# The first input tile of a fused SSM and SwiGLU kernel: one load of 128 rows, or two halves of 64 rows on two DMA queues

## The chip, the cores and the metric

The kernel adds a state space model (SSM) and a gated feed-forward block (SwiGLU) to its input. It runs on one core of a Trainium2 chip. The metric is device time in microseconds (us). "Before" had a median of 179.36 us in three runs (179.34 to 179.51).

The engines are named as in the profile. PE is TensorE (PEld its weight loads), DVE is VectorE, ACT is ScalarE, POOL is GpSimd, and SP is SyncE. A "q" after a name (SPq, ACTq, POOLq) is that engine's instruction queue, from which it also issues DMAs.

## The reference, cut to what matters

```python
def reference(A_x, ..., B_w_gate, B_w_up, B_w_down):
    xn = _layernorm(A_x, axis=-1)          # x is 2048 rows of 512, bf16
    return A_x + _A_ref(xn, ...) + _B_ref(xn, B_w_gate, B_w_up, B_w_down)

def _B_ref(x, w_gate, w_up, w_down):       # 512 -> 1376 -> 512
    return (silu(x @ w_gate) * (x @ w_up)) @ w_down
# _A_ref: a diagonal complex state space scan between two dense projections
```

## The kernel before

The rows are handled in 16 tiles of 128 rows, four to a chunk. Almost all of the time is dense matmul work. This is about the first 13 us, the head. There the first four tiles are loaded, normalised, transposed on TensorE and multiplied with the gate weights one tile ("quarter") at a time, so that TensorE can begin as soon as tile 0 is there.

```python
def x_load(a, **kw):                       # one tile: 128 rows of 1 KB
    return dma("ld_x%d" % a, x_sb[:, a:a + 1, :], x_v[:, a:a + 1, :], [("x", a)], TILEB, **kw)
def wg_load(nm, k0, k1, **kw):             # 128 rows of gate weights per k
    return dma("ld_wg" + nm, wg[:, k0:k1, 0:FG], wg_v[:, k0:k1, 0:FG], [("wg", nm)], ...)

g.add("pool", lambda e: e.memset(prow[:], 0.0), writes=[("prow0",)], name="prow0", est=100)
x_load(0)                                                            # SyncE's queue
x_load(1)
act_q = [dma("ld_touch", tch[0:16], wg_v[0:128:8, :, 0:2], [("tch",)], 16 * 16, eng="act")]
act_q.append(wg_load("a0", 0, 2, eng="act", order=(act_q[-1],)))     # ScalarE's queue
x_load(2)
act_q.append(wg_load("a1", 2, 3, eng="act", order=(act_q[-1],)))
wg_load("a2", 3, 4)
x_load(3)
# ... (parameters, the other weights, tiles 4 to 15)
# PE: 11 warm-up matmuls on constants, transposes of tile 0, 18 gate matmuls
#     of tile 0, transposes of tile 1, ... until 112 are done; then full width
```

The touch reads 256 bytes of the gate weights and nobody uses them. "a0" is the first part of the gate weights (448 KB); the first gate matmul waits for it as well as for tile 0.

## Time and profile before

| what | value | where it is read |
|---|---|---|
| PE busy | 98% of a span of 177.5 us | the page's busy table |
| x tile 0 (x0) complete | 3.10 us | issue at 0.79 plus 2.3 us to landing |
| gate part a0 complete | 5.03 us | issue at 1.23 plus 3.8 us to landing |
| first transposes of tile 0 | 5.00 us | the timeline |
| first gate matmul | 5.83 us | the timeline |
| first full-width gate matmul | 12.94 us | the timeline |

The page has these two lines, the busy time of the engines and the shares of the chain of waits that ended last:

```profile
PE 173.5 (98%) x935; PEld 83.7 (47%) x935; DVE 162.7 (92%) x284; ACT 88.0 (50%) x116; POOL 11.7 (7%) x22
...
PE 96%; DMA 1%; DVE 1%; ACT 1%; issue 0%
```

TensorE bounds the kernel, so only its late start can be shortened. The chain of waits in order of time (columns: start, duration, what) shows that start:

```profile
0.79 2.31 DMA x_sb<-in_A_x_dram
...
3.12 0.71 DVE st L530
...
4.92 0.61 ACT xn_sb L548
...
5.58 0.28 PE pb L582 x2
5.86 0.11 PE pb L477
5.97 1.02 PE pb L803 x18
```

The chain begins with x0's load, goes through the layer norm and then stays on PE. Line 582 is the transposes and line 803 the gate matmuls.

The view of one tile's instructions, narrowed to the first issue, gives the time an issue holds the queue (in ns: minimum, median, maximum) and the time from issue to landing. First x0, then a0:

```profile
L402 SPq DMA_DIRECT2D x_sb<-in_A_x_dram x1: 393/393/393, 0.8 to 0.8; - x1
DMA to landing us min/median/max: 2.3/2.3/2.3
...
L402 ACTq DMA_DIRECT2D wg<-in_B_w_gate_dram x1: 448/448/448, 1.2 to 1.2; - x1
DMA to landing us min/median/max: 3.8/3.8/3.8
```

Issuing x0 holds SyncE's queue for 0.393 us. Gate part a0 is issued at 1.23 us, right behind the touch, and is there 0.8 us before the first gate matmul.

### The profile page before, as it was taken

The numbers are of one execution on the slowest core, as the hardware profiler recorded it, in microseconds if no ns is written. First come the engines' busy times: TensorE is split into PE (matmuls) and PEld (weight loads), VectorE is DVE, ScalarE is ACT, GpSimd is POOL, SyncE is SP. The second block draws the span as 40 slices with busy tenths as digits, with TensorE's granted clock in tenths as the row PEclk, the third lists the DMA queues.
The fourth block names the chain that finished last, engine by engine and source line by source line (L and its number), as shares of the span: only waits on it lengthen the run. The fifth ranks groups of instructions, "written<-read, shape, count | busy, mean of one in ns | idle before, by whom it ended". The sixth has DMA issues, their size and how long they took to land.

```text
span 177.5 us, 2429 instructions
## 1 busy us (share of the span) xinstructions
PE 173.5 (98%) x935; PEld 83.7 (47%) x935; DVE 162.7 (92%) x284; ACT 88.0 (50%) x116; POOL 11.7 (7%) x22
## 2 busy tenths in 40 slices
PE   7899999999999999999999999999999999999994
PEld 3794444444444444444444444444444444444743
DVE  2966999699999999999999999999999999999933
ACT  4679989679999655026565560000965520000000
POOL 3023300040000000260000000000000000000000
PEclk9999999999999999999999999999999999999999
DMA  5994562664946000001520000001000000001022
GB/s 168 311 365 112 118 131 53 170 145 107 352 100 48 0 0 0 0 30 63 110 39 0 0 0 4 0 30 59 30 0 4 0 0 0 0 0 51 11 89 89
DMA packets 23014, 12.37 MB, mean 70 GB/s; under 512 B 15228, under 2 KB 23004, under 8 KB 23004
## 3 DMA queue, kind: packets, MB, share of 16 engines
q1 hardware_dynamic: 22508, 11.54, 24.7%
q10 hardware_dynamic: 496, 0.69, 1.2%
q8 instruction: 7, 0.11, 0.2%
q14 instruction: 3, 0.02, 0.0%
HBM read 6.46 MB, written 2.10 MB: 48 GB/s over the span
## 4 chain that ended last, share of the span: by engine, by line
PE 96%; DMA 1%; DVE 1%; ACT 1%; issue 0%
PE pb L759 36%; PE pb L959 21%; PE pb L972 16%; PE pb L876 16%; PE pb L803 4%; PE pb L839 2%; DMA x_sb<-in_A_x_dram 1%; PE pb L849 1%; PE pb L582 1%; DVE st L530 0%; ACT xn_sb L548 0%; ACT nm L545 0%; ACT sd L524 0%; DVE x_sb L977 0%; DVE mv L522 0%
## 5 line engine op out<-in xcount | busy, mean ns | idle before, releaser
L916 DVE TENSOR_TENSOR_SCAN rot<-sm,car,rot 128x512 bf16<-128x512 f32 x32 | 38.9, 1266 | 0.1
L959 PE MATMUL pb<-wd,hT 128*128 128x512 bf16 (+3 forms) x198 | 38.8, 355 | 0.0
L759 PE MATMUL pb<-xnT,wu 128*128 128x512 bf16 x160 | 37.3, 379 | 0.0
L759 PE MATMUL pb<-xnT,wg 128*128 128x512 bf16 x132 | 31.3, 379 | 0.0
L972 PE MATMUL pb<-W,hss 128*128 128x512 bf16 (+2 forms) x144 | 28.3, 355 | 0.0
L876 PE MATMUL pb<-xnT,BT 128*128 128x512 bf16 x128 | 28.1, 379 | 0.0
L959 PEld LDWEIGHTS pb<-wd,hT 128*128 128x128 bf16 (+1 forms) x198 | 18.5, 98 | 19.9
L759 PEld LDWEIGHTS pb<-xnT,wu 128*128 128x128 bf16 x160 | 15.6, 98 | 18.9 <-issue 0.2
L829 ACT ACTIVATE uf<-pb 128x1024 bf16<-128x1024 f32 x20 | 20.6, 1028 | 7.3 <-PE pb L759 6.1
L771 ACT ACTIVATE sg<-pb 128x1024 bf16<-128x1024 f32 x20 | 20.2, 1025 | 8.0 <-PE pb L759 7.1
L972 PEld LDWEIGHTS pb<-W,hss 128*128 128x128 bf16 x144 | 13.4, 98 | 14.3
L759 PEld LDWEIGHTS pb<-xnT,wg 128*128 128x128 bf16 x132 | 12.7, 98 | 15.7 <-ACT xn_sb L506 0.4
L876 PEld LDWEIGHTS pb<-xnT,BT 128*128 128x128 bf16 x128 | 12.5, 98 | 15.1
L883 ACT ACTIVATE u_sb<-pb 128x1024 bf16<-128x1024 f32 x16 | 16.2, 1019 | 5.7 <-PE pb L876 5.4
L977 DVE TENSOR_TENSOR x_sb<-pb,x_sb 128x512 bf16<-128x512 f32 (+2 forms) x18 | 11.0, 622 | 3.5 <-PE pb L972 3.4
L831 DVE TENSOR_TENSOR hT<-sg,uf 128x1024 bf16<-128x1024 bf16 x20 | 13.4, 681 | 0.0
L506 ACT ACTIVATE xn_sb<-x_sb,nmr,rstd 128x512 bf16<-128x512 bf16 x8 | 6.0, 803 | 9.6 <-DVE nmr L503 9.6
L858 ACT ACTIVATE sg<-pb 96x1024 bf16<-96x1024 f32 x2 | 2.0, 1014 | 17.1 <-PE pb L839 17.1
L482 DVE BATCH_NORM_STATS2 st<-x_sb 128x6 f32<-128x512 bf16 x12 | 7.4, 682 | 3.2 <-DMA x_sb<-in_A_x_dram 3.2
L907 DVE TENSOR_TENSOR rot<-rot,cosT 128x2048 bf16<-128x2048 bf16 x8 | 9.7, 1218 | 0.1
L907 DVE TENSOR_TENSOR rot<-rot,sin 128x2048 bf16<-128x2048 bf16 x8 | 9.8, 1219 | 0.0
L907 DVE TENSOR_TENSOR rot<-u_sb,cosT 128x2048 bf16<-128x2048 bf16 x8 | 9.7, 1218 | 0.0
(81 smaller groups left out, 145.6 us busy)
## 6 DMA issues: line engine op xcount, KB each, us to landing
out_dram<-x_sb SPq DMA_DIRECT2D x15, 128.0 KB, 1.7
x_sb<-in_A_x_dram SPq DMA_DIRECT2D x3, 512.0 KB, 7.4
wd<-in_B_w_down_dram SPq DMA_DIRECT2D x1, 1280.0 KB, 6.9
wu<-in_B_w_up_dram SPq DMA_DIRECT2D x1, 768.0 KB, 5.3
wu<-in_B_w_up_dram SPq DMA_DIRECT2D x1, 608.0 KB, 7.4
x_sb<-in_A_x_dram SPq DMA_DIRECT2D x4, 128.0 KB, 3.6
wg<-in_B_w_gate_dram SPq DMA_DIRECT2D x1, 480.0 KB, 6.2
wg<-in_B_w_gate_dram ACTq DMA_DIRECT2D x1, 448.0 KB, 3.8
```

What stands on the lines that cost most here:

```text
L482: return g.add("dve", lambda e, a=a: e.bn_stats(out=st[:, a, :], in_=x_sb[:, a, :]), reads=[("x", a)], writes=[("st", a)], name="bnst%d" % ...
L759: inst = e.matmul(pbank[0:fs, bk, :].rearrange("p (j t) -> p j t", j=4), lhsT=w[:, kt, i * 128:i * 128 + fs], rhs=xnT[:, c % 2, :, kt, :], ...
L771: g.add("act", lambda e: e.activation(out=sg[rows, sl, 0:n, :].rearrange("p a t -> p (a t)"), in_=pair_f32(rows, bk, 512 * n), func=AF.Sil ...
L829: g.add("act", lambda e: e.activation(out=uf[rows, ul, 0:n, :].rearrange("p a t -> p (a t)"), in_=pair_f32(rows, bk, 512 * n), func=AF.Ide ...
L831: g.add("dve", lambda e: e.tensor_tensor(out=hT[rows, hb, i0:i0 + n, :], in0=sg[rows, sl, 0:n, :], in1=uf[rows, ul, 0:n, :], op=ALU.mult), ...
L876: inst = e.matmul(pbank[:, bk, :].rearrange("p (j t) -> p j t", j=4), lhsT=BT[:, ri, kt, pt * 128:(pt + 1) * 128], rhs=xnT[:, c % 2, :, kt ...
L883: g.add("act", lambda e: e.activation(out=u_sb[:, us].rearrange("p r t -> p (r t)"), in_=pair_f32(slice(0, 128), b0), func=AF.Identity), r ...
L907: tt = lambda out, a, b, op, r, w, nm: g.add("dve", lambda e: e.tensor_tensor(out=out, in0=a, in1=b, op=op), reads=r, writes=w, name="%s_% ...
L916: g.add("dve", lambda e, A0=A0, A1=A1, k=k, ri=ri, pt=pt: e.tensor_tensor_scan(out=A1[:, k, ri, :], data0=rr[:, pt:pt + 1].to_broadcast([1 ...
L959: inst = e.matmul(pbank[:, bk, 0:nc_], lhsT=hT[0:fs, hb, i, lt * 128:(lt + 1) * 128], rhs=wd[0:fs, i, c0:c0 + nc_], start=(i == 0), stop=F ...
L972: inst = e.matmul(pbank[:, bk, 0:nc_], lhsT=hss[:, hb, pt, ri, lt * 128:(lt + 1) * 128], rhs=W12[:, ri, pt, c0:c0 + nc_], start=False, sto ...
L977: g.add("dve", lambda e, bk=bk, a=a, c0=c0, nc_=nc_: e.tensor_tensor(out=x_sb[:, a, c0:c0 + nc_], in0=pbank[:, bk, 0:nc_], in1=x_sb[:, a, ...
```

## The change

The intent is to have x0 sooner: half its rows on each of the two queues, at once. The touch, which held ScalarE's queue first, goes to GpSimd's queue, and GpSimd's constants wait behind it.

```diff
-        g.add("pool", lambda e: e.memset(prow[:], 0.0), writes=[("prow0",)], name="prow0", est=100)
-        x_load(0)
+        tp = dma("ld_touch", tch[0:16], wg_v[0:128:8, :, 0:2], [("tch",)], 16 * 16, eng="pool")
+        g.add("pool", lambda e: e.memset(prow[:], 0.0), writes=[("prow0",)], name="prow0", est=100, order=(tp,))
+        dma("ld_x0", x_sb[0:64, 0:1, :], x_v[0:64, 0:1, :], [("x", 0)], TILEB // 2)
+        act_q = [dma("ld_x0b", x_sb[64:128, 0:1, :], x_v[64:128, 0:1, :], [("x0b",)], TILEB // 2, eng="act")]
         x_load(1)
-        act_q = [dma("ld_touch", tch[0:16], wg_v[0:128:8, :, 0:2], [("tch",)], 16 * 16, eng="act")]
         act_q.append(wg_load("a0", 0, 2, eng="act", order=(act_q[-1],)))
 ... (cut: three more GpSimd memsets get order=(tp,))
-    ... reads=[("x", a)], writes=[("st0", a, 0)] ...
+    ... reads=[("x", a), ("x0b",)], writes=[("st0", a, 0)] ...
```

More of the change, by code (lines that the diff above doesn't have):

```diff
@@ L452, in loads_stage_b2 @@
             dma("ld_dsk", dsk[:], A_Dskip.partition_broadcast(128), [("dsk",)], 128 * 1024)
-        g.add("pool", lambda e: e.memset(epst[:], EPS), writes=[("epst",)], name="epst", est=100)
-        g.add("pool", lambda e: e.memset(mhalf[:], -0.5), writes=[("mhalf",)], name="mhalf", est=100)
-        g.add("pool", lambda e: e.memset(ones[:], 1.0), writes=[("ones",)], name="ones", est=100)
+        g.add("pool", lambda e: e.memset(epst[:], EPS), writes=[("epst",)], name="epst", est=100, order=(tp,))
+        g.add("pool", lambda e: e.memset(mhalf[:], -0.5), writes=[("mhalf",)], name="mhalf", est=100, order=(tp,))
+        g.add("pool", lambda e: e.memset(ones[:], 1.0), writes=[("ones",)], name="ones", est=100, order=(tp,))
         g.add("pool", lambda e: e.affine_select(out=ident[:], in_=ones[:], pattern=[[1, 128]], compare_op=ALU.is_equal,
@@ L529, in bn_full @@
             def bn_full(a, order=()):
-                return g.add("dve", lambda e: e.bn_stats(out=st0[:, a, 0, :], in_=x_sb[:, a, :]), reads=[("x", a)], writes=[("st0", a, 0)], name="bnst%d" % a, est=640, order=order)
+                return g.add("dve", lambda e: e.bn_stats(out=st0[:, a, 0, :], in_=x_sb[:, a, :]), reads=[("x", a), ("x0b",)], writes=[("st0", a, 0)], name="bnst%d" % a, est=640, order=order)
             def recip(a, order):
```

## The prediction

> **What bounds the kernel now.** TensorE. The profile's busy table has PE at 98% of the 177.5 us span; the chain of waits that ended last is 96% PE, and from 5.58 us it is nothing but PE until the last 0.3 us. Only the head can be shortened: x tile 0's load (0.79 to 3.10 us in the chain), DVE/ACT layer norm (3.12 to 5.53), then the first real PE work at 5.58. What is saved there must also be kept by the tiles that follow: PE then consumes x1, x2, x3 and the gate weights as they arrive.
>
> **What the change does, costed from the trace.**
> - x0's load: 128 rows of 1 KB become 64 + 64. In the trace's DMA packet records x0's first packet starts 1.34 us after issue, each of 16 engines moves 8 packets of 46 ns (0.37 us), and the completion packets spread from 2.64 to 2.91 us. Both halves spread over the same 16 engines: no transfer time is saved. The Trainium skill says so ("DMA: Bandwidth & Descriptors", Rules for kernel authors: transfers to disjoint partition halves serialize, don't bother); the packets here agree, x0 already uses all 16. The issue could shrink, but is nearly fixed: 0.41 us for the touch (64 pieces), 0.39 for x0 (128), 0.45 for the first gate load (256). The floor shows too: the 0.2 KB touch takes 2.1 us to land, x0 2.3. Estimate from this: 0.02 to 0.1 us earlier, about 0.04 us of it because the touch's packets (five of 9 ns an engine) leave x0's window.
> - ScalarE's queue: one issue of about 0.4 us replaces another; the gate loads are still issued at about 1.23 and 1.7 us.
> - GpSimd: the memsets, identity and iota move behind the touch, perhaps 1 us later. Identity ends at 1.45 us, used at 4.99; epsilon ends before 1, used at 3.52; the zeroed row precedes the parameter loads at 3.14. Off the path unless the issue holds GpSimd over 2 us.
> - The touch may come with or after the first gate packets (2.90 us), of which some already take 250 to 570 ns against 74 usual. Gate part a0 lands at 5.03, used at 5.8.
> - PE order is unchanged; DVE moves one 4-element op.
>
> **How much is on the path.** x0's gain moves PE's start, but the second transpose pair (6.86 us) starts 0.06 us after DVE finishes x1's normalised half (6.80). That DVE chain holds a statistic of x2, started at 5.93, about when x2 lands (issue 1.66 + 4.2). So x2's arrival is co-critical, and the change adds no bandwidth (DMA share about 1.0 from 4 to 6 us). I expect a short PE wait before x1's transposes to eat most of x0's gain; shuffled packets can move x2 a few tenths either way.
>
> **Predicted:** 179.3 us, range 178.9 to 179.8. Chance of faster by over 2%: 0.01; within 2%: 0.98; slower: 0.01.
>
> **What would show it.** x0's halves landing at 2.95 to 3.1 us; PE's first transposes 0 to 0.15 us earlier; the touch landing at 2.5 to 4 us; the gap before x1's transposes growing by what x0 gained; from 13 us on the same chain, shifted by under 0.3 us.
>
> **What would make it wrong.** GpSimd's issue taking over 2 us, so that epsilon or identity comes late (ACT or PE waiting on POOL, up to 1 us lost); cold gate reads delaying x1, x2 or weights (PE waiting on DMA at 6 to 8 us); a fixed launch cost of GpSimd's queue outside the span; the halves' generation truly running in parallel, with x0 0.3 us sooner and x2 too.

## The result, and the profile after

| | before | changed |
|---|---|---|
| median of 6 runs | 179.44 us | 179.91 us |
| range | 179.29 to 179.65 | 179.58 to 180.31 |
| ratio | | 1.0026 (1.0011 to 1.0041) |

A ratio is the mean time of one kernel's runs over that of the other's in the same rounds, so it is not quite the ratio of the medians. Executions over 1.5% slower than the fastest of the same kernel are left out of the means. A small gain was predicted (179.3 us) and the change lost 0.47 us.

The profile of the changed kernel, the same lines. The page and the chain of waits in order of time:

```profile
PE 174.1 (98%) x927; PEld 84.0 (47%) x935; DVE 162.7 (91%) x284; ACT 87.8 (49%) x116; POOL 9.9 (6%) x23
...
PE 95%; ACTq 1%; ACT 1%; DVE 0%; issue 0%
```

```profile
0.81 0.56 ACTq L402
...
1.41 0.86 ACTq L402
...
2.29 0.49 ACTq L402
...
2.81 1.28 ACT L467
...
4.11 0.29 ACT sm L467
...
5.31 0.37 PE pb L583 x2
...
6.26 0.21 PE pb L478
6.47 1.09 PE pb L804 x18
```

The span grew by 0.5 us, and the chain reaches its first 18 gate matmuls at 6.47 us in place of 5.97: all of the loss is in the head. The chain now begins with ScalarE's queue. Its second issue takes 0.86 us, and ScalarE's table load and first square root come after its issues.

The tile view of the same issues, x0's two halves and then a0:

```profile
L402 SPq DMA_DIRECT2D x_sb<-in_A_x_dram x1: 573/573/573, 0.8 to 0.8; - x1
L402 ACTq DMA_DIRECT2D x_sb<-in_A_x_dram x1: 563/563/563, 0.8 to 0.8; - x1
DMA to landing us min/median/max: 2.2/2.3/2.4
...
L402 ACTq DMA_DIRECT2D wg<-in_B_w_gate_dram x1: 858/858/858, 1.4 to 1.4; - x1
DMA to landing us min/median/max: 4.8/4.8/4.8
```

Half the data takes longer to issue: 0.57 us for each half where the whole tile took 0.39. Gate part a0 is issued 0.18 us later, its issue lasts 0.41 us longer, and it lands at 1.41 + 4.8 = 6.2 us instead of 5.03. Of these 1.17 us, 0.59 had passed when its issue ended. The other 0.58 came after that, and why is not shown (in e9 below, a0 issued late but at the normal speed lost 0.63 there too). The first gate matmul starts at 6.26 us, just behind a0. That alone doesn't show that it waited for a0: it also comes 0.40 us after tile 0's second transposes (5.87 us), as in e1 and e7 below (0.39 and 0.40), where a0 had already landed 0.3 and 1.2 us before. The chain, too, goes through the transposes and not through a0. x0 itself is complete at 3.24 us, not sooner but 0.14 us later.

One more thing differs. TensorE starts at half its clock, and the trace shows the step to full speed in the spacing of equal matmuls (427 ns for 512 columns, then about 217). In the profile of before the clock record has it at 3.52 us. The changed kernel's profile has no clock record, but its spacing stays cold until about 6.5 us. So the first transposes took 0.37 us a pair instead of 0.28. (The profile's PEclk column reads 1.00 where there is no record; it can't be trusted there.) Which part of the loss belongs to the change and which to the moment of the step had to be found out.

### The profile page after: what moved, and what is told of

It reads as the page before. It is cut to its first block, busy times and chain, and to the rows that moved or that the text cites. A ratio compares the mean times of both kernels' runs of the same rounds, so it can differ in the third digit from the quotient of the medians.

```text
span 178.0 us, 2424 instructions
## 1 busy us (share of the span) xinstructions
PE 174.1 (98%) x927; PEld 84.0 (47%) x935; DVE 162.7 (91%) x284; ACT 87.8 (49%) x116; POOL 9.9 (6%) x23
## 4 chain that ended last, share of the span: by engine, by line
PE 95%; ACTq 1%; ACT 1%; DVE 0%; issue 0%
PE pb L760 36%; PE pb L960 21%; PE pb L877 16%; PE pb L973 15%; PE pb L804 4%; PE pb L840 2%; PE pb L850 1%; ACTq L402 1%; PE pb L583 1%; ACT L467 1%; PE pb L478 0%; DVE xn_sb L518 0%; ACT sm L467 0%; DVE x_sb L978 0%; ACT sd L525 0%
## 5 line engine op out<-in xcount | busy, mean ns | idle before, releaser
L960 PE MATMUL pb<-wd,hT 128*128 128x512 bf16 (+3 forms) x194 | 38.1, 355 | 0.2
```

Source lines behind the costliest of these rows:

```text
L960: inst = e.matmul(pbank[:, bk, 0:nc_], lhsT=hT[0:fs, hb, i, lt * 128:(lt + 1) * 128], rhs=wd[0:fs, i, c0:c0 + nc_], start=(i == 0), stop=F ...
```

## The experiments

Three theories were on the table at first. GpSimd theory: its DMA slows the issues of the other queues. Concurrency (pair) theory: two big loads issued at once slow each other. Cold theory: the gate weights' first read is slow, and the touch, now too late, used to hide it. A fourth came up on the way. Shape theory: a load over 64 rows is itself slow to issue. "No touch" below means that no queue reads the touch, so that GpSimd has no DMA at all. All kernels gave correct outputs. Each was run in six executions (e5 in four, e8 in five), beside eleven of before on the same chip.

### Which part of the change costs (e1 to e4, one chip)

e1 is the changed kernel again.

> The changed kernel once more, for a second profile and for its time beside the others on one chip. All theories: ratio 1.001 to 1.004. If the head seen in the first profile is systematic, the issues of x0's halves again take about 0.57 us each, that of the first gate load about 0.86 us, and gate part a0 again lands at about 6.2 us. If it was chance of one execution, these move back towards 0.4, 0.45 and 5 us.

e2 drops the touch from the changed kernel:

```diff
-        tp = dma("ld_touch", ..., eng="pool")        # and every order=(tp,)
```

> Halves on the two queues, no touch read anywhere, GpSimd free of DMA. GpSimd theory (its DMA slows the issues of the other two queues): issues of x0's halves back to about 0.40 us, first gate load's to 0.45, x0 complete by 3.10, time at or below before (ratio 0.998 to 1.000). Concurrency theory (two big loads issued at once slow each other): issues stay near 0.57 us, x0 complete near 3.3, ratio 1.001 to 1.003. Cold theory (the gate weights' first read is slow and the touch hid it): a0 lands later than 5.5 us although the issues are fast, ratio above 1.001.

e3 is before without the touch, so that a0 is ScalarE's first issue; e4 is e3 with the touch first on GpSimd's queue:

```diff
-        act_q = [dma("ld_touch", ..., eng="act")]
+        act_q = []                                   # e3, e4
+        tp = dma("ld_touch", ..., eng="pool")        # e4 only, with order=(tp,) on the memsets
```

> x0 whole on SyncE's queue as before, the touch dropped, so that ScalarE's first issue is the gate load itself, 0.44 us sooner. Cold theory: the first gate packets are slower than in before (more of them over 200 ns) and a0 lands no sooner than 5.0 us, ratio 1.000 to 1.002. GpSimd theory and concurrency theory have nothing against it: GpSimd theory says issues of 0.40 and 0.45 us and a0 at about 4.6 us; concurrency theory says x0's issue, now beside a 448 KB load, is slowed to 0.5 us or more.

> x0 whole on SyncE's queue, the touch on GpSimd, ScalarE starts with the gate load. GpSimd theory: x0's issue slows to about 0.57 us and one of ScalarE's to about 0.8, x0 complete at about 3.3, time above that of the same kernel without touch by 0.2 us or more. Concurrency and cold theories: the same issues and time, within 0.1 us, as the kernel with whole x0 and no touch.

| | x0 | touch | median us | ratio (95%) | x0's issues us | a0's issue us |
|---|---|---|---|---|---|---|
| e1 | row halves | GpSimd | 180.08 | 1.0049 (1.0027 to 1.0070) | 0.576, 0.540 | 0.595 |
| e2 | row halves | none | 179.92 | 1.0031 (1.0009 to 1.0053) | 0.575, 0.565 | 0.859 |
| e3 | whole | none | 179.52 | 1.0010 (0.9994 to 1.0027) | 0.396 | 0.465 |
| e4 | whole | GpSimd | 179.57 | 1.0010 (0.9994 to 1.0026) | 0.398 | 0.468 |

The GpSimd theory falls twice. The issues are slow without any DMA on GpSimd (e2) and fast with it (e4). GpSimd issued the touch from 1.35 us on for 0.741 us, in e4 as in the changed kernel. The issues of x0's halves, which began at 0.80, were thus nearly over when it began. Here is e4's tile view over SyncE's first two issues, of which the second overlaps with the touch:

```profile
L402 SPq DMA_DIRECT2D x_sb<-in_A_x_dram x2: 398/406/413, 0.8 to 1.3; - x2
```

The cold theory falls with e3. Without any touch a0 landed at 4.63 us, 3.84 us after its issue, as long as in before (3.80), and 8 of the first 256 packets on its queue took over 200 ns, against 11 in before and 7 in e12, before's repeat. Concurrency in its plain form falls too: in e3 and e4 x0 (128 KB) and a0 (448 KB) were issued at the same moment and neither was slowed. What is left is the cut into 64 rows.

In e1 SyncE's queue lost, which its expectation hadn't foreseen: the issue of x tile 1 (x1) took 0.817 us and x1 landed at 5.83 us (3.85 in the first profile). In e2 it was ScalarE's: 0.859 us for a0. So the loss takes two roads so far, late gates or a late x1. In e1 the late x1 stopped TensorE by way of ScalarE: its square root for x1 (at 6.89 us) stood ahead of its copy of tile 0's second half, and TensorE waited 0.49 us for that copy. A third road, tile 0's own path, is shown under the table of the heads.

### Pair or shape (e5 to e8, one chip)

e5 puts both halves on SyncE's queue, with the touch on ScalarE's as before:

```diff
-        x_load(0)
+        dma("ld_x0", x_sb[0:64, ...], ...)           # SyncE
+        dma("ld_x0b", x_sb[64:128, ...], ...)        # SyncE
```

> Both 64-row halves on SyncE's queue one after the other, the touch on ScalarE's as before. Shape theory (a 64-row load is itself slower to issue than a 128-row one): both issues about 0.57 us, x0 complete at 3.6 us or later. Pair theory (only two halves issued at the same moment slow each other): issues of about 0.38 us each, x0 complete at about 3.35, the gate loads' issues as in before (0.45 us), a0 landing near 5.0; time 0.2 to 0.4 us above before either way, because one more issue of SyncE goes ahead of x1.

e6 loads x0 whole, and reads 64 rows of it a second time into a scratch tile in place of the touch:

```diff
-        act_q = [dma("ld_touch", tch[0:16], ..., eng="act")]
+        act_q = [dma("ld_touch", xs[64:128], x_v[64:128, 0:1, :], ..., eng="act")]
```

> x0 whole (128 rows) on SyncE's queue; ScalarE's first issue is a 64-row read of the same tile into a scratch tile in place of the touch. Shape theory: ScalarE's issue 0.57 us, SyncE's 0.39. Pair theory in the form 'two reads of one tile at once': both slow, 0.5 us or more. Pair theory in the form 'two equal 64-row loads': neither slow, 0.39 to 0.41 us. The time is above before by 0.1 to 0.5 us whichever holds (64 KB more to move ahead of the gates).

e7 cuts x0 by columns, with no touch:

```diff
-        dma("ld_x0", x_sb[0:64, 0:1, :], ...);  dma("ld_x0b", x_sb[64:128, 0:1, :], ..., eng="act")
+        dma("ld_x0", x_sb[:, 0:1, 0:256], ...); dma("ld_x0b", x_sb[:, 0:1, 256:512], ..., eng="act")
```

> x0 in two column halves (128 rows of 512 bytes each) on the two queues at once, no touch. Shape theory: issues 0.39 to 0.42 us as every 128-row load, x0 complete by about 3.2, gates in time, ratio 0.999 to 1.001. Pair theory (two loads of one tile at once): issues 0.5 us or more, one of the two queues' second issue 0.8 us, ratio 1.002 to 1.005 as with the row halves.

e8 keeps row halves but puts the touch ahead of the upper one on ScalarE's queue, so that the halves are not issued together:

```diff
+        act_q = [dma("ld_touch", ..., eng="act")]
-        act_q = [dma("ld_x0b", ..., eng="act")]
+        act_q.append(dma("ld_x0b", ..., eng="act", order=(act_q[-1],)))
```

> Lower half first on SyncE's queue, and on ScalarE's the touch first and then the upper half, about 0.45 us behind. Shape theory: each half's issue is about 0.57 us though they no longer start together, SyncE's first one too. Pair theory: about 0.39 us for the first half (beside the touch) and 0.40 for the second (beside x1). x0 complete at 3.4 to 3.6 us; ratio 1.001 to 1.004 either way.

| | median us | ratio (95%) | issue of the half, us | next issue on its queue, us |
|---|---|---|---|---|
| e5 both on SyncE | 183.43 | 1.0240 (1.0223 to 1.0258) | 0.580, then 0.578 | 0.578 (x1) |
| e6 64 rows on ScalarE, x0 whole | 180.92 | 1.0095 (1.0059 to 1.0131) | 0.543 (x0 whole: 0.393) | 0.593 (a0) |
| e7 column halves | 179.28 | 1.0007 (0.9995 to 1.0019) | 0.394 and 0.393 | 0.424 (x1), 0.475 (a0) |
| e8 row halves, apart | 179.93 | 1.0048 (1.0036 to 1.0060) | 0.581 and 0.546 | 0.565 (x1), 0.597 (a0) |

The shape theory predicted all of the first issues rightly, and the pair theory fell. A 64-row load took 0.54 to 0.58 us alone beside the touch (e5), beside a whole tile (e6), and apart from its partner (e8). A 128-row load of half as many bytes a row took 0.39 at the same moment as its twin (e7). The load behind a 64-row load on the same queue was slow too: about 0.57 us for x1 against 0.41, about 0.6 for a0 against 0.45. Only where both queues started with 64 rows at once did one of the next issues reach 0.82 to 0.86 us. The times agree: e8 and e7 stood on one chip, and their intervals don't overlap. Nor do those of e7 and e11 below (another chip), which differ only in the cut, columns or even and odd rows, both without a touch.

Two sizes were missed widely. e6 lost 1.8 us where 0.1 to 0.5 was expected: a0 landed at 7.46 us, 6.1 us after its issue, its 16 landings spread from 5.09. The cause of that spread is open. e5 lost 4.3 us. Its second half was issued behind a0. Its packets moved only from about 3.9 us on, when most of a0's had moved, and it landed at 5.29. The chain of waits of e5 in order of time:

```profile
1.43 3.87 DMA x_sb<-in_A_x_dram
...
8.45 1.92 PE pb L804 x18
```

The 18 gate matmuls took 1.92 us instead of 1.02, because in this execution TensorE's clock record reaches full speed only at 13.36 us. A late tile was paid for twice, once as a wait and once as a slow clock.

### Late gates, what makes the shape slow, and a null (e9 to e12, one chip)

e9 leaves x0 whole and issues three touches ahead of a0 instead of one:

```diff
+        for k_ in range(2):
+            act_q.append(dma("ld_touch%d" % k_, tch[0:16, k_], ..., eng="act", order=(act_q[-1],)))
```

> Before with three touch reads in place of one on ScalarE's queue, x0 whole: nothing changes but that the gate parts a0 and a1 are issued about 0.87 us later. If late gate weights are what costs the time in the changed kernel, a0 lands at 5.8 to 6.2 us, the first gate matmul starts about 0.05 us after it, and the time rises by 0.2 to 0.6 us with x0 complete near 3.1. If the lateness of x0 is what costs, the time stays within 0.1 us of before.

e10 loads rows 0 to 63 of tiles 0 and 1 in one load, and rows 64 to 127 of both in another, with no touch:

```diff
-        dma("ld_x0", x_sb[0:64, 0:1, :], ...);  dma("ld_x0b", x_sb[64:128, 0:1, :], ..., eng="act"); x_load(1)
+        dma("ld_x0", x_sb[0:64, 0:2, :], ...);  dma("ld_x0b", x_sb[64:128, 0:2, :], ..., eng="act")
```

> Rows 0 to 63 of tiles 0 and 1 in one load on SyncE's queue, rows 64 to 127 of both on ScalarE's, no touch: 64 rows, but 128 pieces of 1 KB each. If the number of SBUF rows makes the issue slow, each still takes 0.55 us or more. If it is the number of pieces (64 instead of 128), the issue is back at about 0.40 us. x0 and x1 complete together at about 3.5 us, so PE starts about 0.4 us later, but with one SyncE issue fewer ahead of x2; ratio 1.001 to 1.005.

e11 takes even and odd rows for the halves, with no touch:

```diff
-        x_sb[0:64, 0:1, :]      x_sb[64:128, 0:1, :]
+        x_sb[0:128:2, 0:1, :]   x_sb[1:128:2, 0:1, :]
```

> x0 in two halves of 64 rows on the two queues at once, even rows and odd rows, no touch. If a half is slow to issue because its 64 rows are one contiguous piece of DRAM and of SBUF, the issues are back at 0.40 us and the time at before's, ratio 0.999 to 1.001. If 64 rows as such are slow, 0.57 us again and ratio 1.002 to 1.005.

e12 is before, unchanged.

> The kernel before, once more, as a null and for a second profile: ratio 0.999 to 1.001. All theories need its issues at 0.39 to 0.45 us, a0 at about 5.0 us and x0 at about 3.1 us again; the moment at which TensorE goes to full speed may be another.

- e9: 181.26 us, ratio 1.0112 (1.0073 to 1.0150). x0 was complete at 3.06 us as in before, a0 at 6.61, and the first gate matmul came at 6.75; the chain of waits goes through a0's DMA. The profiled execution took 180.21 us, 0.93 above that of before, as much as the first gate matmul was later (0.92). The test isn't pure: ScalarE's longer queue also held back its table load (3.18 us instead of 2.23) and its first square root, so that the second transposes came at 6.17 instead of 5.58. This accounts for 0.59 of the 0.92 us, and the wait for the late gates for the other 0.33. Three of its six runs lay at 182 to 182.4, beyond what was expected.
- e10: 180.44 us, ratio 1.0087 (1.0057 to 1.0116). The issues took 0.737 and 0.700 us for 128 pieces in 64 rows, against 0.39 to 0.41 for 128 pieces in 128 rows. The slow shape isn't a matter of few pieces.
- e11: 180.23 us, ratio 1.0059 (1.0042 to 1.0076). Issues of 0.587 and 0.559 us, so it isn't a matter of one contiguous block either. Here SyncE's queue lost (0.824 us for x1, landing at 5.49) while a0 came at 5.11, in time: the second of the two roads, with a loss of 1.0 us.
- e12: 179.48 us, ratio 1.0010 (0.9996 to 1.0024). The noise of one such comparison is thus 0.1 to 0.15%. The head repeated: x0 at 3.13, a0 at 4.98, first gate matmul at 5.85.

e10's profile holds the clearest record of the clock. Its clock record steps to full at 3.51 us, back to half at 6.92 and to full again at 10.34. Four windows cut there (columns: window, then its length and the busy time of PE, PEld, DVE, ACT, POOL with the number of instructions, then PEclk, DMA share, GB/s); the 1.00 of the first window is missing data, as said above:

```profile
0.10:3.51 3.41, 2.68 (x7) 1.02 (x8) 0.00 (x0) 0.83 (x1) 1.49 (x13) 1.00 0.36 101
3.51:6.92 3.41, 1.41 (x12) 0.63 (x9) 2.15 (x7) 2.25 (x8) 0.00 (x0) 1.00 0.95 312
6.92:10.34 3.42, 3.42 (x34) 3.37 (x33) 2.22 (x10) 1.30 (x6) 0.00 (x0) 0.50 1.01 333
10.34:13.75 3.41, 3.41 (x64) 3.37 (x62) 2.26 (x9) 2.20 (x6) 1.02 (x1) 1.00 1.03 339
```

PE was busy for only 1.41 of 3.41 us in the second window, and in the third its clock was half: 34 matmuls where the fourth window has 64. The Trainium skill ("TensorE: Matmul & The Clock Gate", Part 1) says that the clock follows activity in a free-running window of 3413 ns, and that the moment of the step depends on where in the window a kernel starts. The three steps here, 3.41 and 3.42 us apart, agree. Over the profiled executions of all these kernels the first step was recorded anywhere from 3.51 to 6.26 us, and once at 13.36. It moved between executions of one kernel too: 6.14 and 3.64 us in two of the changed kernel's. We take that as luck of the execution, not the change, as long as the wait for tile 0 stays short. A longer wait can cost a whole window, as in e5 and e10. That would explain runs such as e9's at 182, but only e5's and e10's profiles show it.

### The shape alone, in the changed kernel (e13 to e16)

Row and column halves had been timed on different chips with different touches. e13 and e15 are the changed kernel with nothing altered but the cut; e14 and e16 are the changed kernel beside them.

```diff
-        dma("ld_x0", x_sb[0:64, 0:1, :], x_v[0:64, 0:1, :], ...)        # upper rows on ScalarE
+        dma("ld_x0", x_sb[:, 0:1, 0:256], x_v[:, 0:1, 0:256], ...)      # columns 256:512 on ScalarE
```

> The changed kernel with nothing altered but the cut: x0 in two halves of 256 columns (128 rows of 512 bytes) in place of 64 rows, same queues, touch still on GpSimd. Shape theory: issues 0.39 to 0.42 us, the first gate load's about 0.47, x0 complete at about 3.25, a0 by 5.0; ratio 0.999 to 1.002. If something else in the change also costs (the queue pair, the touch on GpSimd), the ratio stays at 1.002 or more though the issues are fast.

> The changed kernel on the same chip: ratio 1.002 to 1.006, issues of the halves about 0.57 us, one of the two next issues 0.8 us or more, and late either the gates (ScalarE's queue loses) or x1 (SyncE's loses).

> The changed kernel with column halves again, because the first try was taken on a disturbed chip. Shape theory: issues 0.39 to 0.47 us, x0 complete near 3.15, a0 by 5.1, ratio 0.999 to 1.001, and below the row halves' on the same chip by 0.001 to 0.004. If something else in the change costs too, the two stand within 0.001 of each other, both at 1.002 or more.

> The changed kernel (row halves) beside it: ratio 1.002 to 1.005, issues near 0.57 us, one of the two next issues over 0.8 us, a0 landing near 6.1 us if ScalarE's queue loses, x1 near 5.8 us if SyncE's does.

The first try was inconclusive: e13 was 1.0001 (0.9977 to 1.0025) and e14 1.0009 (0.9986 to 1.0033). On that chip even the fast runs of before spread from 179.12 to 180.31.

The second try: e15 had a median of 179.55 us and a ratio of 1.0021 (1.0003 to 1.0039); e16 had 179.75 us and 1.0053 (1.0011 to 1.0096), with one run at 182.23; before had 179.26. The averages order as the shape theory says, but the intervals overlap and e15 isn't free of loss. The profiles tell more, because by luck the clock stepped at nearly the same moment in both, 4.40 us in e15 and 4.46 in e16. The tile view of x0's halves and of a0, first e15 (columns):

```profile
L402 SPq DMA_DIRECT2D x_sb<-in_A_x_dram x1: 393/393/393, 0.8 to 0.8; - x1
L402 ACTq DMA_DIRECT2D x_sb<-in_A_x_dram x1: 398/398/398, 0.8 to 0.8; - x1
DMA to landing us min/median/max: 2.2/2.2/2.3
...
L402 ACTq DMA_DIRECT2D wg<-in_B_w_gate_dram x1: 463/463/463, 1.2 to 1.2; - x1
DMA to landing us min/median/max: 3.8/3.8/3.8
```

Then e16 (rows), the same view:

```profile
L402 SPq DMA_DIRECT2D x_sb<-in_A_x_dram x1: 575/575/575, 0.8 to 0.8; - x1
L402 ACTq DMA_DIRECT2D x_sb<-in_A_x_dram x1: 565/565/565, 0.8 to 0.8; - x1
DMA to landing us min/median/max: 2.3/2.4/2.5
...
L402 ACTq DMA_DIRECT2D wg<-in_B_w_gate_dram x1: 859/859/859, 1.4 to 1.4; - x1
DMA to landing us min/median/max: 5.0/5.0/5.0
```

And e16's chain of waits in order of time:

```profile
0.81 0.56 ACTq L402
...
1.41 4.97 DMA wg<-in_B_w_gate_dram
...
6.43 1.25 PE pb L804 x18
```

With the clock out of the comparison, the chain of the row halves goes straight through a0's DMA. In e15 the chain goes through x0 instead, with a0 landing in time at 5.0 us:

```profile
0.80 2.33 DMA x_sb<-in_A_x_dram
...
3.16 0.02 DVEq L244
...
3.23 0.70 DVE st L531
...
6.14 1.02 PE pb L804 x18
```

The first full-width gate matmul came at 13.00 us in e15 and 13.52 in e16: 0.51 us apart, in two profiled executions that differ only in the cut. The first gate matmul was 0.43 us later in e16. Of this, 0.20 came with tile 0's second transposes (5.95 instead of 5.75 us) and 0.23 was the wait for a0.

### One table of the heads

Times within the span, from the profiled executions. The step is from the clock record, or, with "~", from the spacing of matmuls where the record is missing.

| kernel | x0 complete | x1 complete | a0 complete | clock step | first gate matmul | first full-width | run us |
|---|---|---|---|---|---|---|---|
| before | 3.10 | 4.35 | 5.03 | 3.52 | 5.83 | 12.94 | 179.28 |
| changed | 3.24 | 3.85 | 6.20 | ~6.5 | 6.26 | 13.40 | 179.73 |
| changed, e14 | 3.23 | 3.71 | 6.06 | 3.64 | 6.12 | 13.12 | 179.45 |
| changed, e16 | 3.33 | 3.84 | 6.38 | 4.46 | 6.43 | 13.52 | 179.83 |
| changed, e1 | 3.23 | 5.83 | 5.85 | 6.14 | 6.16 | 13.93 | 180.54 |
| rows, no touch, e2 | 3.31 | 3.91 | 6.38 | 5.82 | 6.43 | 13.63 | 179.97 |
| columns, e15 | 3.13 | 3.76 | 5.00 | 4.40 | 6.00 | 13.00 | 179.40 |
| columns, no touch, e7 | 3.25 | 3.65 | 4.96 | ~6.7 | 6.12 | 13.58 | 179.93 |
| whole, e4 | 3.35 | 4.92 | 4.59 | ~6.2 | 6.17 | 13.25 | 179.61 |
| late a0, e9 | 3.06 | 3.69 | 6.61 | 4.91 | 6.75 | 13.90 | 180.21 |

The last two columns differ by 166.3 to 166.4 us in every row but e1's (166.6). Nothing after the head gives back or adds to what the head lost, with that one exception. The row of e7 warns against reading single rows: issues and gates were fast there, and still its first full-width matmul is 0.64 us behind before's. Most of that, 0.50 us between tile 0's second transposes and tile 1's first, goes with the late clock, and the median of e7's six runs (ratio 1.0007) doesn't show it.

The cleanest look at the change itself is e14 beside before, because the clock stepped at 3.64 and 3.52 us (one execution of each). Here is e14's chain of waits in order of time:

```profile
1.41 0.86 ACTq L402
...
2.82 1.28 ACT L467
...
4.88 0.30 ACT nm L546
...
5.87 0.28 PE pb L583 x2
6.15 0.11 PE pb L478
6.26 1.02 PE pb L804 x18
```

It goes through ScalarE and tile 0's transposes, not through a0. The second transposes came 0.29 us later than in before (5.87 and 5.58), and so did the first gate matmul. Of this, 0.13 is x0's later landing. Another 0.08 lies between landing and statistics: VectorE now waits for two loads, and its second wait is an instruction of its own (DVEq L244, in e15's chain above), which costs time when the half that it waits for lands last (in e1 and e2, where the other half did, landing and statistics are 0.02 us apart as in before). The remaining 0.08 came in ScalarE's steps: 0.03 before its first square root for x0, which stood behind a table load that began at 2.82 us instead of 2.23, and 0.05 after it. Gate part a0 landed at 6.06, 0.06 us before the first gate matmul. So tile 0 and the gates were late together in the changed kernel, and it changed from one execution to the next which of them held TensorE: in e16 a0 did, by 0.23 us, in e14 it was a tie.

## Why the prediction was wrong, point by point

- **TensorE bounds the kernel and only the head can move: right.** The loss is in the first 13 us, and the rest keeps its length.
- **"The issue could shrink, but is nearly fixed": wrong, and this is the step that failed.** It was sized from loads over 16 and 128 rows. A load over 64 rows takes 0.54 to 0.59 us to issue against 0.39, and slows the issue behind it on the same queue.
- **"ScalarE's queue: one issue of about 0.4 us replaces another; the gate loads are still issued at about 1.23 and 1.7 us": wrong for the same reason.** The half took 0.563 us and a0 0.858, so the two gate loads were issued at 1.41 and 2.29. Gate part a0, called slack by 0.8 us, landed 1.17 us later. All of its slack was gone: it tied with tile 0 in two profiles of the changed kernel and was what the first gate matmul waited for in e16.
- **x0 0.02 to 0.1 us sooner, complete by 3.1 us: wrong in sign.** It was complete at 3.23 to 3.33 us in the profiles of the changed kernel. No transfer time is saved, as said; what was gained by halving was negative. Fast issues would not have brought the gain either: with column halves x0 was complete at 3.13 us in e15 and 3.25 in e7. The prediction also left out what waiting for two loads costs (0.08 us in e14).
- **The packet times quoted were 0.31 us too late,** because their origin was misread. In the span's time x0's first packet is at 1.82 us, 1.03 us after issue, and its completion packets are at 2.33 to 2.60. The counts and durations (8 packets of 46 ns) stand, and the conclusion doesn't rest on the origin.
- **x2 co-critical, and x0's gain eaten before x1's transposes: moot.** There was no gain to eat. What bound instead was tile 0's own path, a0 or, in e1 and e11, x1.
- **GpSimd off the path: right.** Its issue held it until 2.08 us, and the identity was ready at 2.77, used at 5.3. With x0 whole the touch on GpSimd changed the median by 0.05 us (e3, e4). The touch landed at 3.89 to 4.92 us (predicted 2.5 to 4) and nobody missed it.
- **The warning of "cold gate reads" had the right place and the wrong cause.** The gates came late behind slow issues, not because the touch was missing (e3).

The chance of "within 2%" (0.98) was borne out; the centre was off by 0.6 us, because the one term taken as constant was the one that grew. The experiments' own expectations were mostly right on the issues but too low on the time: e1, e5, e6, e8, e9, e10, e11, e15 and e16 all lost more than was expected (e10 1.0087 against at most 1.005).

Open are why 64 rows are slow to issue (no other row count between 16 and 128 was tried), and why one of two queues then takes 0.82 to 0.86 us for its next issue. The Trainium skill ("Perfetto Trace Analysis", DMA Instruction — HWDGE) describes a descriptor generator that is locked for exclusive use, with the wait for it inside the reported span of an issue. That would fit the second, but no run here separates such a wait, and two 128-row loads issued at the same moment (e7, e15) took 0.39 to 0.40 us each, with none to be seen. None of the versions tried beats before.

## What to carry to other kernels

Time the issue of every load shape that you introduce, not its bytes: a load that moves half as much can hold its queue half as long again, and the load queued behind it pays. When a change puts something in front of a queue, follow the next two loads on that queue to their first use, and the engine's own first instructions too, if the queue is that of a computing engine; here the weights behind the tile, and ScalarE's table load behind its issues, came as late as the tile that was to come sooner. Count one more wait for each load that a tile is cut into. If a first tile has to be cut over two queues, a cut by columns that keeps all 128 rows issued at the normal speed here, though even that gained nothing over one whole load.

## What the Trainium skill lacked or had wrong

- "DMA: Bandwidth & Descriptors", Rules for kernel authors: it says that two transfers to disjoint partition halves serialize and that one shouldn't bother. The runs agree that nothing is gained, but the page lacks that it can cost: 0.54 to 0.59 us to issue 64 rows against 0.39 to 0.41 us for 128, and 0.57 to 0.86 us for the load behind instead of 0.41 to 0.45.
- The same page, Issuing engines are not separate DMA queues: it says that the sequencer time of an issue is usually small relative to the DMA. Here the issue is 0.39 us of the 2.3 us that x0 takes to land, and slower issues made 0.59 of the 1.17 us by which the gates were late.
- No page gives the issue time on the SyncE or ScalarE queue of this chip by load shape. These runs show 0.39 us (128 rows of 512 bytes or 1 KB), 0.57 us (64 rows of 1 KB), 0.70 to 0.74 us (64 rows with two pieces of 1 KB each).
- "TensorE: Matmul & The Clock Gate", Part 1: the free-running window is confirmed (steps at 3.51, 6.92 and 10.34 us in e10). The page says that the transition comes around 4 us into sustained activity, give or take 0.5 us; here, with warm-up matmuls from 0.83 us on, the first step was recorded from 3.51 to 6.26 us, that is 2.7 to 5.4 us after the first matmul, and at 13.36 us where the first tile was late (e5).
